# Re-timing one block's attention chunks and moving small products off VectorE in a retention and two-layer MoE kernel on one Trainium2 core

## The chip, the core and the metric

The kernel runs on one core of one Trainium2 chip. The metric is the device time of one execution in microseconds (us); lower is better. Profiles come from the hardware profiler and show one execution.

## What is computed

The reference is a chain of three parts over 4 sequences of 768 tokens with 8 heads of 64. First a retention layer: a state that decays by gamma per token and per head.

```python
state = gamma * state + outer(k[t], v[t])
y[t] = scale * (q[t] @ state)
```

Its result, 3072 tokens by 512, goes through a first layer (512 to 2048 to 512) whose activation is a cubic in h over a positive quadratic in h and |h|, and then through a second layer of the same sizes whose activation is h * clip(h + 3, 0, 6) / 6. All of it is float32 in and out.

## The kernel before, in words

The tokens are cut into 6 blocks of 512, and each block into 4 chunks of 128. A chunk is written (block, chunk) here, so (2,0) is the first chunk of the third block, which the code calls `VIA`. Every matrix product of the two layers is made of three products of rounded parts (a high part and a low rest, `h` and `l` in the names), 12 matmuls of 512 columns for the first product of a step and 12 for the second.

**Steps.** The main loop (lines 703 to 766) has one step for each block and each of 16 slices of 128 hidden features. Step n issues, among other things, on TensorE the first product h of step n (`emit_h`, line 356), then the second product of step n-2 (`emit_o`, line 368), then attention work that is hung behind it (`after`). Here they are called h(n) and o(n-2). On ScalarE (ACT) it issues the three readings of h(n-1) (`s1_h`, lines 437 to 439), the rounding of the finished activation to its high part gh(n-2) (line 467), the work on weights, then a logarithm and an exponential for h(n-1) (lines 454, 455). On VectorE (DVE) it issues the last three operations of the activation of n-2 (lines 460 to 462), weight bits (lines 125, 126), three operations on h(n-1) with the low part gl(n-2) among them (lines 445, 446, 473, 449), and attention work (`before`). Steps 0 to 7 belong to block 0, steps 8 to 23 to block 1, steps 24 to 31 again to block 0, and step 32 begins block 2. Each engine issues its instructions in the order of the program; the order between engines follows from semaphores that the tile framework sets.

**Attention chunks.** A chunk passes through: five transfers into on-chip tiles (`att_load`, line 201: q, the table for q, k, v, and k by rows, in this order), q times the table on DVE (`att_q`, line 215), v times a per-head power (`att_v`, line 220, whose result is called v' here), scores on TensorE (line 233), a mask on DVE (line 244), outputs and the state's sum on TensorE (lines 269 to 304), and evacuation on ACT and DVE (lines 327 or 332, 339, 344 or 346). `chunk_at` (line 586) hangs them on steps, for a score step s:

```python
put(before, loads, att_load, blk, c)
put(before, s - 1, att_q, blk, c)
put(before, s - 1, att_v, blk, c)
put(after, s, att_scores, blk, c)
put(before, s + 1, att_mask, blk, c)
put(after, s + 1, att_out, blk, c)
```

The second block's scores stand at steps -1, 1, 3 and 5 and those of the third block at steps 8, 12, 16 and 20, with their transfers two steps earlier (line 601). From the third block on, a chunk's q, k and v lie in the tiles `T`, `kv` and `tq` (lines 191 to 194), of which there is one each. So the transfers of the next chunk wait for the last reader of the chunk before, and the SyncE queue (SP), which issues them in the program's order, stands still meanwhile. The chunks of the third block leave by way of DRAM (`x_dram`, line 328) and are loaded back before step 32.

**Weights.** The 64 weight tiles of both layers are loaded raw, scaled on ACT (line 117), turned on DVE (lines 125, 126), rounded to the high part on ACT (line 134), and the low rest is made in one of two ways: a subtraction on DVE (line 146), or a negated copy on ACT (line 138) and a transfer issued by GpSimd (POOL) that adds the raw tile to it (line 144). `SUMS` (line 22) says which tiles take the second way, counted from 0 in the order of their use: 3 to 25 and 32 to 39. `w_until` (line 534) sets how many tiles are made by the end of a step: two a step up to step 7, then about four in five steps; tiles 26 to 31 fall in steps 16 to 22. A raw tile's room is loaded again as soon as its low rest is made (`w_ahead`, line 543).

**Evacuation.** The sum of a block (or of the first half of block 0) is copied out by ACT in four pieces (line 418) into tiles that have three buffers, and stored; the fourth copy waits for the first store. For block 0's first half this is in step 10.

Of the kernel before, what the change touches and what calls it, by code (L numbers as in the profile page):

```python
# [11 lines left out]
AF = mybir.ActivationFunctionType  # L12
ALU = mybir.AluOpType
# [3 lines left out]
NB = 512  # L17
EARLY = (0, 1)
VIA = 2
CUT1, CUT2 = 8, 8  # L20
LAG = 2
SUMS = ((3, 26), (32, 40))
EARLY_AT = 8
SPARE = ("wi14", "wi15", "wo14", "wo15")
WARM, WARM_AGAIN = 3, 3
# [6 lines left out]
def tile_retention_moe_moe2(  # L32
# [13 lines left out]
    nc = tc.nc  # L46
    NT, DM = out.shape
    H, D, S = N_HEADS, DM // N_HEADS, SEQ
# [4 lines left out]
    CPB = NB // CH  # L53
    CPS = S // CH
# [19 lines left out]
    tab_v = [tab[:, CH + i * H : CH + (i + 1) * H] for i in range(CPS)]  # L74
# [142 lines left out]

    def att_v(blk, c):
        vr = attn[blk, c][3]
        nc.vector.tensor_tensor(  # L220
            out=vr,
            in0=vr,
            in1=tab_v[(blk * CPB + c) % CPS].unsqueeze(2).to_broadcast([128, H, D]),
            op=ALU.mult,
        )

    def att_scores(blk, c):
        qT, kT, kr, vr, ka = attn[blk, c]
# [93 lines left out]
    def att_xh(blk, c):  # L322
        y = attn[blk, c][0].rearrange("p (e j t) -> p e j t", e=2, t=CH)[:, :, 0:2, :]
        xs = slice(c * CH, (c + 1) * CH)
        if blk == VIA:
            xf = o_p.tile([128, 512], F32, tag="osb", name=f"xf{blk}_{c}")
# [7 lines left out]
    def att_xl(blk, c):  # L334
        both = attn[blk, c][0]
        if blk != VIA:
            y = both.rearrange("p (e j t) -> p e j t", e=2, t=CH)[:, :, 0:2, :]
# [193 lines left out]
    def by_dma(i):  # L531
        return any(lo <= i < hi for lo, hi in SUMS)

# [49 lines left out]
    def put(where, n, fn, *args):  # L583
        where.setdefault(n, []).append((fn, *args))

    def chunk_at(blk, c, s, loads=None):
        if loads is not None:
# [7 lines that stand above are left out]
        s += blk == VIA  # L595
        put(middle if blk <= VIA else begin, s + 2, att_xh, blk, c)
        put(before, s + 2, att_evac, blk, c)

    for c in range(CPB):
        chunk_at(1, c, 2 * c - 1, max(2 * c - 3, -1))  # L600
        chunk_at(VIA, c, CUT1 + 4 * c, CUT1 - 2 + 4 * c)
        for b in range(VIA + 1, NBLK):
            n0 = at_of[0, b - 1, 0] if b > VIA + 1 else 2 * FT
            chunk_at(b, c, n0 + 4 * c, n0 + 4 * c - 2)
# [47 lines left out]
    att_q(0, 0)  # L652
    att_scores(0, 0)
    att_v(0, 0)
    att_mask(0, 0)
    att_out(0, 0)
    att_q(0, 1)
    att_scores(0, 1)
    keep_warm(WARM_AGAIN)
    att_v(0, 1)  # L660
    att_state(0, 0)
    att_xh(0, 0)
# [175 lines left out]
```

## Time and profile before

| | us |
|---|---|
| median of 3 runs | 1172.44 (1170.27 to 1173.0) |
| the profiled execution's own time | 1170.62 |
| its span, first to last instruction | 1168.8 |

The profiled execution is 1.8 us under the median, and 1.8 us of it lie outside its span. In the timeline a row is: start in us, length in us, engine, line and operation, tile written and tiles read, count of merged instructions, and in brackets the idle time of the engine before it and what ended it. Lengths of matmuls are modelled and reach into the next row by about 0.15 us, so the time that a group takes is read from the start of one group to the start of the next.

### The profile page before, as it was taken

Reading aid. Unit: us, or ns where it says so; the run is one execution under the profiler, and the core shown is the slowest. Engines: PE = TensorE matmul, PEld = TensorE weight load, DVE = VectorE, ACT = ScalarE, POOL = GpSimd, SP = SyncE. Lnnn points to the kernel's source line nnn. Section 1 sums busy time; section 2 is a strip of 40 time slices with the busy share of each in tenths; the row PEclk is TensorE's granted clock in tenths of the full one; section 3 lists DMA queues with packets and bytes.
Section 4 is the critical chain, followed back from the end, with each engine's and each line's share of the span. In section 5 each row is a group of like instructions: output and inputs, shape, how many; then the busy total and the mean of one; then the engine's idle time right before and its main releaser. Section 6 shows DMA issues by size and latency. Waiting matters only on the chain.

```text
span 1168.8 us, 15667 instructions
## 1 busy us (share of the span) xinstructions
PE 1142.8 (98%) x6028; PEld 929.6 (80%) x6028; DVE 762.1 (65%) x1187; ACT 625.3 (53%) x1029; POOL 27.6 (2%) x37
## 2 busy tenths in 40 slices
PE   8699999999999999999999999999999999999998
PEld 5567787888888888888888788888888888888886
DVE  6898999998888878888899865432332332332322
ACT  3788876866666666666888644332232332232222
POOL 0121000000000000000000000000000000000000
PEclk9899999999999999999999999999999999999999
DMA  9898722311112113121332743120200200200000
GB/s 335 244 263 231 189 67 63 135 60 68 46 46 82 46 59 113 47 81 37 109 99 64 231 134 105 36 90 1 73 1 1 72 1 1 72 1 1 36 1 36
DMA packets 58683, 98.62 MB, mean 84 GB/s; under 512 B 5233, under 2 KB 23793, under 8 KB 58609
## 3 DMA queue, kind: packets, MB, share of 16 engines
q1 hardware_dynamic: 54144, 89.50, 23.2%
q0 software_dynamic: 4464, 8.13, 4.2%
q8 instruction: 47, 0.77, 0.3%
q14 instruction: 28, 0.22, 0.1%
HBM read 73.76 MB, written 15.73 MB: 77 GB/s over the span
## 4 chain that ended last, share of the span: by engine, by line
PE 77%; DVE 11%; ACT 6%; DMA 3%; issue 3%; SPq 0%; ACTq 0%; DVEq 0%
PE h L365 37%; PE accA L389 19%; PE accB L389 18%; DMA T<-in_qk_t_dram 2%; DVE u L460 2%; DVE p L461 1%; DVE p L445 1%; PE sc L233 1%; PE py L269 1%; ACT r L454 1%; DVE u L446 1%; ACT r L455 1%; DVE p L449 1%; DVE p L462 1%; DVE rwo L126 1%
## 5 line engine op out<-in xcount | busy, mean ns | idle before, releaser
L365 PE MATMUL h<-xh,wi 128*128 128x512 f32 x1536 | 416.5, 393 | 0.9 <-ACT xh L332 0.9
L365 PEld LDWEIGHTS h<-xh,wi 128*128 128x128 f32 x1536 | 285.6, 188 | 64.0 <-issue 3.0
L365 PE MATMUL h<-xl,wi 128*128 128x512 f32 x768 | 206.1, 390 | 0.0
L485 DVE SCALAR_TENSOR_TENSOR g<-r,h 128x512 f32<-128x512 f32 x96 | 66.0, 688 | 169.0 <-ACT r L479 168.4
L365 PEld LDWEIGHTS h<-xl,wi 128*128 128x128 f32 x768 | 144.5, 188 | 31.1 <-DVE xl L339 0.3
L479 ACT ACTIVATE r<-h,cst 128x512 f32<-128x512 f32 x96 | 66.0, 687 | 183.3 <-PE h L365 182.7
L473 DVE TENSOR_TENSOR gl<-g,gh 128x512 fp32r<-128x512 f32 x96 | 66.5, 693 | 120.6 <-ACT gh L467 120.6
L467 ACT ACTIVATE gh<-g 128x512 fp32r<-128x512 f32 x96 | 60.7, 632 | 153.1 <-PE accB L389 113.9
L389 PE MATMUL accA<-gh,wo 128*128 128x512 f32 x384 | 120.5, 395 | 7.3 <-ACT gh L467 7.3
L389 PE MATMUL accB<-gh,wo 128*128 128x512 f32 x384 | 119.3, 392 | 0.0
L389 PE MATMUL accA<-wo,gh 128*128 128x512 f32 x384 | 118.2, 389 | 0.0
L389 PE MATMUL accB<-wo,gh 128*128 128x512 f32 x384 | 118.2, 389 | 0.0
L437 ACT ACTIVATE p<-h,ab 128x512 f32<-128x512 f32 x96 | 74.3, 774 | 37.6 <-PE h L365 35.4
L454 ACT ACTIVATE r<-u,cst 128x512 f32<-128x512 f32 x96 | 69.3, 722 | 43.5 <-DVE u L446 43.4
L389 PEld LDWEIGHTS accA<-gh,wo 128*128 128x128 f32 x384 | 71.4, 189 | 26.1 <-ACT gh L467 11.8
L473 DVE TENSOR_TENSOR gl<-p,gh 128x512 fp32r<-128x512 f32 x96 | 65.9, 687 | 31.0 <-ACT gh L467 30.8
L389 PEld LDWEIGHTS accB<-gh,wo 128*128 128x128 f32 x384 | 72.6, 189 | 15.4
L389 PEld LDWEIGHTS accA<-wo,gh 128*128 128x128 f32 x384 | 72.1, 188 | 15.0
L389 PEld LDWEIGHTS accB<-wo,gh 128*128 128x128 f32 x384 | 72.1, 188 | 15.0
L467 ACT ACTIVATE gh<-p 128x512 fp32r<-128x512 f32 x96 | 60.7, 632 | 38.8 <-DVE p L462 38.8
L389 PE MATMUL accA<-wo,gl 128*128 128x512 f32 x192 | 74.7, 389 | 0.0
L389 PE MATMUL accB<-wo,gl 128*128 128x512 f32 x192 | 74.7, 389 | 0.0
(74 smaller groups left out, 1418.4 us busy)
## 6 DMA issues: line engine op xcount, KB each, us to landing
rwi<-in_moe_w_in_dram SPq DMA_DIRECT2D x32, 512.0 KB, 4.8
rwo<-in_moe_w_out_dram SPq DMA_DIRECT2D x32, 512.0 KB, 3.7
T<-in_qk_t_dram SPq DMA_DIRECT2D x48, 256.0 KB, 4.1
kv<-in_kv_dram SPq DMA_DIRECT2D x32, 256.0 KB, 4.8
x<-o SPq DMA_DIRECT2D x24, 256.0 KB, 2.3
xr<-x SPq DMA_DIRECT2D x24, 256.0 KB, 4.1
out_dram<-o SPq DMA_DIRECT2D x20, 256.0 KB, 2.0
wi<-rwi POOLq DMA_DIRECT2D x17, 256.0 KB, 3.9
```

Source lines behind the costliest of these rows:

```text
L126: nc.vector.scalar_tensor_tensor(out=z, in0=hw, scalar=3, in1=lw, op0=ALU.logical_shift_left, op1=ALU.bitwise_or)
L233: nc.tensor.matmul(banks[e][:, p * CH : (p + 1) * CH], lhsT=kT[rows, p, :], rhs=qT[rows, p, :], start=True, stop=True)
L269: nc.tensor.matmul(to(e, j, i), lhsT=vr[:, 2 * p + e, :], rhs=am[:, e * NP + p, :], start=j == 0, stop=first and j == 1, skip_group_check= ...
L365: nc.tensor.matmul(ps, lhsT=w[:, cs], rhs=x[:, c, :], start=n == 0, stop=n == 3 * KD - 1)
L389: nc.tensor.matmul(acc[layer, blk][j], lhsT=l, rhs=r, start=f == f0 and i == 0, stop=f == f1 and i == 2)
L437: nc.scalar.activation(p, h, AF.Identity, scale=ab[:, 3:4], bias=ab[:, 2:3])
L454: nc.scalar.activation(r, u, AF.Ln, scale=1.0 / LN_SCALE, bias=ln_bias)
L460: nc.vector.scalar_tensor_tensor(out=u, in0=u, scalar=Q_CONST, in1=r, op0=ALU.add, op1=ALU.mult)
L467: nc.scalar.activation(gh, tm[key], AF.Copy)
L473: nc.vector.tensor_tensor(out=gl, in0=tm.pop(key), in1=gh.bitcast(F32), op=ALU.subtract)
L479: nc.scalar.activation(r, hps[key], AF.Relu, bias=three)
L485: nc.vector.scalar_tensor_tensor(out=g, in0=r, scalar=6.0, in1=h, op0=ALU.min, op1=ALU.mult)
```

## The change

Three things change. The third block's scores go from steps 8, 12, 16, 20 to steps 10, 13, 16, 20, and everything that `chunk_at` hangs on them with them: transfers from steps 6, 10, 14, 18 to 8, 11, 14, 18. The product v' of the seven chunks (1,1) to (2,3) is made on ACT by eight operations of 64 columns with a per-partition scale, in place of one operation of 512 columns on DVE; it is issued at the same place in the step. And weight tiles 26 to 31 (the 27th to the 32nd) take the way by negated copy and adding transfer.

```diff
+VIA_AT = (10, 13, 16, 20)
...
-SUMS = ((3, 26), (32, 40))
+SUMS = ((3, 40),)
...
     def att_v(blk, c):
         vr = attn[blk, c][3]
-        nc.vector.tensor_tensor(
-            out=vr,
-            in0=vr,
-            in1=tab_v[(blk * CPB + c) % CPS].unsqueeze(2).to_broadcast([128, H, D]),
-            op=ALU.mult,
-        )
+        powers = tab_v[(blk * CPB + c) % CPS]
+        if (1, 0) < (blk, c) < (VIA + 1, 0):
+
+            for h in range(H):
+                nc.scalar.activation(vr[:, h, :], vr[:, h, :], AF.Copy, scale=powers[:, h : h + 1])
+        else:
+            nc.vector.tensor_tensor(
+                out=vr, in0=vr, in1=powers.unsqueeze(2).to_broadcast([128, H, D]), op=ALU.mult
+            )
...
-        chunk_at(VIA, c, CUT1 + 4 * c, CUT1 - 2 + 4 * c)
+        chunk_at(VIA, c, VIA_AT[c], VIA_AT[c] - 2)
```

## Rows read from the trace of the kernel before

**Rows 1.** The page, busy time of engines over the span.

```profile
PE 1142.8 (98%) x6028; PEld 929.6 (80%) x6028; DVE 762.1 (65%) x1187; ACT 625.3 (53%) x1029; POOL 27.6 (2%) x37
```

**Rows 2.** Windows: stretch, length, busy time by engine, granted clock, DMA share, GB/s.

```profile
50.00:100.00 50.00, 43.45 (x288) 32.90 (x288) 49.19 (x80) 43.75 (x76) 10.53 (x12) 0.98 0.97 249
...
150.00:200.00 50.00, 49.40 (x300) 39.68 (x300) 47.75 (x77) 34.96 (x58) 0.00 (x0) 1.00 0.20 59
```

**Rows 3.** Timeline of TensorE: waits, scores of (2,0), and o(8) before h(11).

```profile
34.27 1.09 PE L269 MATMUL py<-T,T 128*64 128x128 f32 x16 [1.76 <-DVE T L244]
...
98.18 1.08 PE L389 MATMUL accA<-gh,wo 128*128 128x512 f32 x2 [2.85 <-ACT gh L467]
...
102.72 1.16 PE L233 MATMUL sc<-T 64*128 64x128 f32 x16
103.81 1.19 PE L365 MATMUL h<-xh,wi 128*128 128x512 f32 x4
...
114.43 0.62 PE L389 MATMUL accA<-gh,wo 128*128 128x512 f32 x2
...
117.15 1.07 PE L365 MATMUL h<-xh,wi 128*128 128x512 f32 x4
...
126.08 0.73 PE L389 MATMUL accA<-gh,wo 128*128 128x512 f32 x2 [0.61 <-ACT gh L467]
...
187.86 1.09 PE L269 MATMUL py<-T,kv 128*64 128x128 f32 x16 [0.60 <-DVE T L244]
...
203.87 0.73 PE L389 MATMUL accA<-gh,wo 128*128 128x512 f32 x2 [0.48 <-ACT gh L467]
```

**Rows 4.** Windows after two of these waits: granted TensorE clock is third from the end.

```profile
34.27:38.00 3.73, 2.15 (x48) 1.85 (x48) 3.21 (x6) 2.17 (x5) 1.06 (x1) 1.00 0.67 176
...
98.40:101.70 3.30, 3.30 (x9) 2.52 (x9) 2.38 (x4) 3.24 (x6) 0.86 (x1) 0.50 0.91 222
```

**Rows 5.** Timeline of VectorE in step 7: v' of (2,0), then weight bits.

```profile
91.87 0.69 DVE L220 TENSOR_TENSOR kv<-kv,tab 128x512 f32<-128x512 f32 x1
...
93.86 0.69 DVE L126 SCALAR_TENSOR_TENSOR rwo<-rwo 128x512 int32<-128x512 int32 x1
```

**Rows 6.** Timeline of ScalarE in steps 7 to 10.

```profile
94.58 0.63 ACT L134 ACTIVATE wo<-rwo 128x512 fp32r<-128x512 f32 x1 [0.97 <-DVE rwo L126]
...
106.91 0.76 ACT L437 ACTIVATE p<-h,ab 128x512 f32<-128x512 f32 x1
...
108.62 1.09 ACT L418 ACTIVATE o<-accA 128x512 f32<-128x512 f32 x2
...
112.00 0.60 ACT L418 ACTIVATE o<-accB 128x512 f32<-128x512 f32 x1 [1.80 <-DMA x<-o]
112.49 0.62 ACT L467 ACTIVATE gh<-p 128x512 fp32r<-128x512 f32 x1
```

**Rows 7.** Timeline of ScalarE: the narrowest operations with a per-partition scale.

```profile
5.30 2.43 ACT L208 ACTIVATE T<-T,T 128x128 f32<-128x128 f32 x8
```

**Rows 8.** Timeline of TensorE: outputs of (2,2), and h(18) after them.

```profile
161.65 1.09 PE L269 MATMUL py<-T,kv 128*64 128x128 f32 x16
...
163.74 1.20 PE L365 MATMUL h<-xh,wi 128*128 128x512 f32 x4
```

**Rows 9.** Timeline of the SyncE queue: q and v of (2,3).

```profile
163.87 0.33 SPq L201 DMA_DIRECT2D T<-in_qk_t_dram  x1
...
165.24 0.86 SPq L201 DMA_DIRECT2D kv<-in_kv_dram  x2
```

**Rows 10.** DMA issues, 138 to 141, then 163.5 to 166.5: count, KB, us to landing.

```profile
kv<-in_kv_dram SPq DMA_DIRECT2D x2, 256.0 KB, 6.3
...
kv<-in_kv_dram SPq DMA_DIRECT2D x2, 256.0 KB, 4.2
```

**Rows 11.** Line 201 from 80 to 260 us, 28 transfers.

```profile
DMA to landing us min/median/max: 2.6/4.4/7.1
```

**Rows 12.** Waits: ScalarE's scaling for weight loads, whole span.

```profile
ACT rwo L117 <- DMA rwo<-in_moe_w_out_dram: 2.4, 3, 1.2
```

**Rows 13.** Groups by line: the subtraction that makes a low rest.

```profile
L146 DVE TENSOR_TENSOR wo<-rwo,wo 128x512 fp32r<-128x512 f32 x18 | 12.4, 690 | 7.1 <-ACT wo L134 7.1
```

## The prediction

> **What bounds the kernel now.** I read the page first: TensorE (PE) is busy 1143 of 1169 us [rows 1], so the end moves only where PE waits, or where PE's clock falls. Then windows, to find where that is. Between 50 and 100 us VectorE (DVE) is busy 49.2 of 50 us and PE only 43.5, while ScalarE (ACT) has 6.2 us free; between 150 and 200 us PE is busy 49.4 of 50 [rows 2]. So up to about step 8 DVE sets the pace, and later PE does. Then PE's timeline, step by step. The dearest place is o(6) in step 8: PE waits 2.85 us for gh(6), and the group up to the scores behind it then takes 98.18 to 102.72, 4.54 us, where o(8) takes 114.43 to 117.15, 2.72 us [rows 3]. In that stretch the granted clock is 0.50, the lower level of 1.2 GHz; after a wait of 1.76 us at 34.27 it stayed at 1.00 [rows 3, 4]. So this wait costs 2.85 and 1.8 more. Behind step 10 only three waits of weight are left, 0.61, 0.60 and 0.48 us [rows 3]. What I had to see in each view: how little there is to win after step 10, and that new PE waits there count in full.
>
> Why o(6) is late: in step 7 DVE makes q and v' of (2,0), about 0.6 us each from start to start, before the weight bits; ACT waits 0.97 us for these bits and only then gets to h(7) and gh(6) [rows 5, 6].
>
> **What the change does, part by part.** It is followed through the two in-order queues of ACT and DVE by the starts of the rows.
>
> *Steps 0 to 8.* Three v' leave DVE, 0.6 us each. ACT gets eight operations for each. Eight of 128 columns took 2.43 us with the last one's tail, 0.29 apart [rows 7]; a copy of 512 columns is 0.49 apart from the next [rows 6], so most of an operation is fixed. With 64 columns I take 0.24, so 1.9 us for a v' (bounds 0.15 and 0.29: 1.2 and 2.3). ACT's free time swallows most of that; I leave DVE a lead of 0.75 at step 7 (bounds 0 and 1.8). There q and v' of (2,0) go too: 1.2. So the bits come 2.0 earlier, and o(6) starts at 96.2 instead of 98.18. PE then waits about 1.8 us, as at 34.27, where the clock did not fall. o(6) ends at 98.9 instead of 102.7.
>
> *Steps 8 to 10.* The scores of (2,0), 1.09 us, and its outputs, 2.09 us as for (2,2) [rows 3, 8], leave steps 8 and 9 and come in 10 and 11. That is 3.2 us of PE work which stood where PE could wait and now stands where it can't. Meanwhile v' of (2,0) is queued on ACT in step 9, in front of the readings of h(9). These started at 106.91; 2.0 earlier by the lead and 1.9 later by v' makes 106.8. Behind them ACT copies out four pieces from 108.62, the fourth waits for the first one's store, and gh(8) follows at 112.49 [rows 6]. Nothing shortens that, so gh(8) starts at 112.4 and o(8) at 113.0, where it was 114.43. PE is 1.4 us earlier with 3.2 us more to do: **+1.8**. PE has nothing from about 109.2 to 113.0. That gap of 3.8 is nearest to the 2.85 after which the clock fell, so I take another half-speed stretch: **+1.8** (bounds 0 and 1.8). The wait of 0.61 at 126.08 is covered by that lateness: **-0.6**.
>
> *The transfers of (2,1) and (2,2).* This is the part that decides. Before, a chunk's outputs came three steps ahead of the next chunk's v'. In the new spacing of three steps, the outputs of (2,0) are at the end of step 11, the transfers of (2,1) are issued in step 11 too, and q and v' of (2,1) are wanted in step 12. With one `T` and one `kv` tile, the transfer must wait for those outputs: for (2,3) the q transfer is issued at 163.87, 0.13 us after PE had finished the outputs of (2,2) [rows 8, 9]. v is issued 1.37 us behind q, and lands 4.2 to 6.3 us later [rows 9, 10]. From the end t of PE's step 11 then: v there at t + 5.7 to 7.8; v' on ACT, 1.9; the readings of h(12), which are queued behind it, 1.71; gh(11), 0.63 [rows 6]: t + 9.9 to 12.0. PE does h(12), o(10) and h(13) meanwhile, 3 x 2.72 = 8.16 us, and then needs gh(11) for o(11). It waits 1.8 to 3.9 us; I take the middle, 2.8. DVE's q waits too (q and its table land earlier) but comes through in time. The same holds for (2,2): outputs of (2,1) at the end of step 14, v' in step 15, wait before o(14): **+5.6** for the two (bounds 3.6 and 7.8). Whether the clock falls again after waits of 2.8 I leave to the upper end, 1.8 each: the shorter ends lie at the 1.76 that left it alone. (2,3) keeps its steps.
>
> *Queues.* While SP stands at these transfers, weight loads and the stores of the third block stand behind them, a few us. I cost this at nothing, since loads run ahead of their use: ACT waited for one three times in the whole kernel, 2.4 us in all [rows 12]. If that cover were gone, SP's 2.2 us of five issues would come on top. In turn the transfers of (2,0) move back two steps and let weight loads go first.
>
> *Weight tiles.* Six subtractions of 0.69 us leave DVE in steps 16 to 23 [rows 13]; ACT gets six copies of the same size, where it is busy 35 of 50 us [rows 2], and POOL, 2% busy [rows 1], six transfers. No weight is loaded into the freed rooms before step 80, and each tile is first used some steps later. On the path lie only the waits of 0.60 and 0.48 [rows 3]: **-1.1** (bounds -1.1 and 0).
>
> Sum: 1.8 + 1.8 - 0.6 + 5.6 - 1.1 = **+7.5 us** on the profiled execution, 1170.62 to 1178.1. That execution is 1.8 under the median of the runs, so I put the difference on the median: 1172.44 + 7.5 = **1179.9**. All low bounds together, with v' at 1.2 us in its three places, give about +1.6; all high ones, with the clock, +16.
>
> One rule speaks for a smaller sum. In the rows, a 256 KB transfer issued behind two others took 4.2 to 6.3 us to land, and the shortest of 28 took 2.6 [rows 10, 11]. The Trainium skill, page "DMA: Bandwidth & Descriptors", section "Anatomy of one DMA — SWDGE (gpsimd) path", puts a transfer at about 2 us plus its bytes at 436 GB/s, which would be an estimate of 2.6 us here; by it each wait would be 0.2 and the sum +2.3. The trace agrees with it in its shortest row only.
>
> **Rivals.** *Transfers land quickly* (within 0.3%). With 2.6 us, v is there at t + 4.1, each wait shrinks from 2.8 to 0.2, and the sum to +2.3: **1174.7**. For it: DMA is 20% busy after 150 us, against 97% before 100 [rows 2]. Against: both rows for v, the slower one at 138, in the same stretch.
>
> *DVE's relief carries, and ACT takes v' where it waits anyhow* (faster). Place: ACT in steps 9, 12 and 15. Then o(7) ends at 98.9 + 5.4 = 104.3, the four copies start there, gh(8) follows 3.9 later and o(8) starts at 108.9: 5.5 earlier with 3.2 more to do, -2.3; no fall of the clock; -0.6 and -1.1 as above; and the first steps give DVE's whole 1.8 instead of 0.75, -1.1. Together -5.1: **1167.3**. It decides when v' of (2,0) takes none of ACT's path and v of (2,1) lands within 2.4 us, which no row shows. For it: DVE is the fuller engine, and ACT has 6.2 us free.
>
> *The waits are long and the clock falls each time* (slower still). Landings of 6.3 and a half-speed stretch behind each of the two waits: 7.5 + 2 x 1.1 + 2 x 1.8 = +13.3: **1185.7**.
>
> That the change does not do what it says is no case of its own: the order on each engine is the program's. Only the weight part may do nothing, and that is in its bounds.
>
> **How the numbers follow.** What this kernel's measurement can tell from no change is about 0.3%, 3.5 us. Forecast (+3.5 to +10) 0.48; longer waits 0.16; quick landings, or errors that cancel, 0.15; faster 0.21. So slower 0.64, same 0.15, faster 0.21. The range from 1167 to 1186 takes in all named cases and leaves out about 2 in 10 of what lies beyond them; the likeliest case's own range is 1176 to 1183.
>
> **What would show it.** Right: in the new trace o(6) starts about 2 us earlier without a stretch at 0.50 behind it; eight small ACT operations end shortly before the readings of h(9); PE waits for gh(8) 3 to 4 us; SP issues q of (2,1) and (2,2) right behind the outputs of the chunk before; and ACT's first v' operation in steps 12 and 15 waits for a transfer of v, with PE waiting 2 to 4 us before o(11) and o(14). Wrong: if v' there does not wait for its transfer, if PE has no wait before o(11) and o(14), or if a v' takes ACT under 1 us.

## The result and the profile after

The changed kernel takes 1184.64 us (median of 4 runs, 1181.92 to 1187.8) beside 1171.59 us for the kernel before in the same session (1170.27 to 1173.0): 1.0107 times as long, 95% interval 1.0094 to 1.0119, so 12 to 13 us slower. The forecast was slower, 1179.9 us in a range from 1167 to 1186. The time lies in the range, but above the likeliest case's own range (1176 to 1183, chance 0.48) and nearest to the third rival, long waits with the clock falling behind each (chance 0.16). The profiled execution spans 1180.0 us against 1168.8, which is 11.2 more. It is the fastest of the four; the other three took 2.3 to 5.9 us longer, at a mean granted clock of 0.988 to 0.990 instead of 0.991, and they have no trace.

The page's line of engines answers [rows 1]:

```profile
PE 1148.2 (97%) x6028; PEld 933.8 (79%) x6028; DVE 754.6 (64%) x1174; ACT 641.0 (54%) x1091; POOL 32.7 (3%) x43
```

DVE lost 7.5 us of work and ACT won 15.7, as the change says, and the kernel got slower all the same. PE's busy time rose by 5.4 us with the same 6028 instructions: some of them ran at half clock. So the difference has two parts, waits of PE and clock, and both are to be read in PE's timeline, which answers [rows 3]. After 94 us it holds these waits of over 0.1 us, and no other up to 260:

```profile
97.39 0.73 PE L393 MATMUL accA<-gh,wo 128*128 128x512 f32 x2 [1.77 <-ACT gh L471]
...
105.45 0.50 PE L393 MATMUL accA<-gl,wo 128*128 128x512 f32 x1 [1.53 <-DVE gl L477]
...
114.30 0.73 PE L393 MATMUL accA<-gh,wo 128*128 128x512 f32 x2 [1.96 <-ACT gh L471]
...
136.86 0.96 PE L393 MATMUL accA<-gh,wo 128*128 128x512 f32 x2 [2.16 <-ACT gh L471]
...
161.97 1.22 PE L393 MATMUL accA<-gh,wo 128*128 128x512 f32 x2 [3.26 <-ACT gh L471]
```

They stand before o(6), the gl part of o(7), o(8), o(11) and o(14), together 10.7 us. The kernel before has waits of 2.85, 0.61 and 0.15 up to 175 us, together 3.6. The windows that begin at each of these five rows give the clock behind it (columns as in [rows 2], granted clock third from the end):

```profile
97.39:104.00 6.61, 6.47 (x26) 4.72 (x26) 5.62 (x10) 6.13 (x11) 0.86 (x1) 1.00 1.03 302
105.45:110.00 4.55, 4.55 (x13) 3.64 (x14) 4.32 (x8) 4.52 (x14) 0.58 (x1) 0.62 0.98 256
114.30:120.00 5.70, 5.70 (x35) 4.55 (x36) 3.96 (x7) 5.22 (x10) 0.86 (x1) 1.00 0.70 187
136.86:142.00 5.14, 5.14 (x22) 3.93 (x24) 5.07 (x10) 4.22 (x8) 0.00 (x0) 0.67 0.55 157
161.97:169.00 7.03, 7.03 (x29) 5.30 (x30) 5.88 (x11) 6.55 (x12) 0.86 (x1) 0.58 0.35 75
```

What the clock costs in a window is estimated as its length times (1 - granted clock): 0.38 x 4.55 = 1.7 us behind o(7), 1.7 behind o(11), 3.0 behind o(14), and nothing behind o(6) and o(8). Why o(11) and o(14) are late, SP's queue and ACT show:

```profile
126.38 0.33 SPq L202 DMA_DIRECT2D T<-in_qk_t_dram  x1
...
127.70 0.91 SPq L202 DMA_DIRECT2D kv<-in_kv_dram  x2
...
150.36 0.34 SPq L202 DMA_DIRECT2D T<-in_qk_t_dram  x1
...
151.70 1.44 SPq L202 DMA_DIRECT2D kv<-in_kv_dram  x2
```

```profile
106.12 2.01 ACT L225 ACTIVATE kv<-kv,tab 128x64 f32<-128x64 f32 x8
108.03 0.76 ACT L441 ACTIVATE p<-h,ab 128x512 f32<-128x512 f32 x1
...
113.13 0.60 ACT L422 ACTIVATE o<-accB 128x512 f32<-128x512 f32 x1 [1.84 <-DMA x<-o]
...
132.55 2.03 ACT L225 ACTIVATE kv<-kv,tab 128x64 f32<-128x64 f32 x8 [2.71 <-DMA kv<-in_kv_dram]
...
157.66 2.02 ACT L225 ACTIVATE kv<-kv,tab 128x64 f32<-128x64 f32 x8 [5.92 <-DMA kv<-in_kv_dram]
```

In PE's timeline, h(12) and h(15) begin at 126.24 and 150.23, and the groups behind o(11) and o(14) (scores, then h) follow:

```profile
126.24 1.20 PE L369 MATMUL h<-xh,wi 128*128 128x512 f32 x4
...
141.39 1.16 PE L237 MATMUL sc<-T 64*128 64x128 f32 x16
...
150.23 1.20 PE L369 MATMUL h<-xh,wi 128*128 128x512 f32 x4
...
168.71 1.19 PE L369 MATMUL h<-xh,wi 128*128 128x512 f32 x4
```

So PE goes on with h(12) and with h(15) right behind the outputs of (2,0) and of (2,1); 0.14 and 0.13 us later SP issues q of the next chunk. v follows 1.3 us behind q, and ACT's first v' operation ends a wait for it of 2.71 and 5.92 us: v was there 4.9 and 6.0 us after its issue. From there 4.31 us pass to o(11) and to o(14), both times (132.55 to 136.86, 157.66 to 161.97). ACT never waited for a weight load here, so what the prediction costed at nothing, loads standing behind these transfers, did cost ACT nothing.

### The profile page after: what moved, and what is told of

Same layout as the page of the kernel before. It is cut to its first block, busy times and chain, and to the rows that moved or that the text cites. A ratio compares the mean times of both kernels' runs of the same rounds, so it can differ in the third digit from the quotient of the medians.

```text
span 1180.0 us, 15740 instructions
## 1 busy us (share of the span) xinstructions
PE 1148.2 (97%) x6028; PEld 933.8 (79%) x6028; DVE 754.6 (64%) x1174; ACT 641.0 (54%) x1091; POOL 32.7 (3%) x43
## 4 chain that ended last, share of the span: by engine, by line
PE 79%; DVE 8%; ACT 7%; DMA 3%; issue 2%; SPq 0%; ACTq 0%; DVEq 0%
PE h L369 37%; PE accA L393 19%; PE accB L393 19%; DMA T<-in_qk_t_dram 2%; PE sc L237 1%; PE py L273 1%; DVE u L464 1%; DVE p L465 1%; DVE p L449 1%; ACT r L458 1%; DMA kv<-in_kv_dram 1%; DVE u L450 1%; ACT r L459 1%; PE py L301 1%; DVE p L453 1%
## 5 line engine op out<-in xcount | busy, mean ns | idle before, releaser
L393 PEld LDWEIGHTS accB<-gh,wo 128*128 128x128 f32 x384 | 73.7, 192 | 15.7
L449 DVE TENSOR_TENSOR p<-p,h 128x512 f32<-128x512 f32 x96 | 65.5, 682 | 23.2 <-ACT u L443 23.2
```

Of the source, the lines that this page charges most:

```text
L393: nc.tensor.matmul(acc[layer, blk][j], lhsT=l, rhs=r, start=f == f0 and i == 0, stop=f == f1 and i == 2)
L449: nc.vector.tensor_tensor(out=p, in0=p, in1=h, op=ALU.mult)
```

## The experiments

The first four, of one session, undo one part or do one part alone; the kernel before took 1172.64 us in it. The rest ran in two later sessions (before: 1172.58 and 1171.96), so across sessions the ratios are compared.

### e1_steps_back: the change without the new steps

```diff
-VIA_AT = (10, 13, 16, 20)
+VIA_AT = (8, 12, 16, 20)
```

> The changed kernel with the third block's steps put back to 8, 12, 16, 20; v' on ScalarE and the weight tiles by transfer stay. My theory (the steps cost, by the transfers of (2,1) and (2,2) that wait for the outputs of the chunk before): no wait on a v transfer in front of ScalarE's v', TensorE waits before o(11) and o(14) under 0.7 us, and the time is within 3 us of the kernel before. Rival (56 small operations on ScalarE cost by themselves, seven times 1.9 us): the time stays at least 8 us over the kernel before.

1170.28 us (1169.26 to 1172.75), ratio 0.9983 (0.9973 to 0.9993). No wait for a transfer of v is left, and PE's timeline holds these two waits after 94 us:

```profile
99.19 0.74 PE L393 MATMUL accA<-gh,wo 128*128 128x512 f32 x2 [3.50 <-ACT gh L471]
...
127.85 0.73 PE L393 MATMUL accA<-gh,wo 128*128 128x512 f32 x2 [1.36 <-ACT gh L471]
```

So v' on ACT and the weight tiles together are worth 0.2%, and all of the loss needs the steps. The first wait, before o(6), is longer than the 2.85 of [rows 3]; e3_v_only shows it again.

### e2_steps_only: the kernel before with the new steps

```diff
-        chunk_at(VIA, c, CUT1 + 4 * c, CUT1 - 2 + 4 * c)
+        chunk_at(VIA, c, VIA_AT[c], VIA_AT[c] - 2)
```

> The kernel before with only the third block's steps moved to 10, 13, 16, 20; v' stays on VectorE, the sums as before. My theory: VectorE now stands before v' of (2,1) and (2,2) until v lands, 5.7 to 7.8 us after the outputs before; then v' 0.6, three operations 2.0 and gh 0.7, so TensorE waits 1 to 3 us before o(11) and before o(14), with half clock behind some of these waits: 4 to 9 us over the kernel before. Rival (v' on ScalarE is what costs): at most 1 us over it.

1179.88 us (1178.05 to 1182.81), ratio 1.0063 (1.004 to 1.0086). With v' on DVE, it is DVE that waits for v, and PE's waits before o(11) and o(14) follow, each 3.40 us after v' began:

```profile
132.93 0.69 DVE L221 TENSOR_TENSOR kv<-kv,tab 128x512 f32<-128x512 f32 x1 [1.93 <-DMA kv<-in_kv_dram]
...
154.94 0.69 DVE L221 TENSOR_TENSOR kv<-kv,tab 128x512 f32<-128x512 f32 x1 [2.51 <-DMA kv<-in_kv_dram]
```

```profile
136.33 0.73 PE L390 MATMUL accA<-gh,wo 128*128 128x512 f32 x2 [1.61 <-ACT gh L468]
...
158.34 0.73 PE L390 MATMUL accA<-gh,wo 128*128 128x512 f32 x2 [1.75 <-ACT gh L468]
```

The windows behind both show a clock of 1.00, so the half clock that I expected behind some of these waits did not come:

```profile
136.33:142.00 5.67, 5.67 (x35) 4.51 (x36) 5.60 (x10) 5.02 (x9) 0.00 (x0) 1.00 0.58 179
158.34:164.00 5.66, 5.50 (x33) 4.05 (x34) 5.63 (x10) 5.02 (x9) 0.00 (x0) 1.00 0.17 46
```

Most of the loss is in the steps by themselves, and there is more of it when v' is on ACT: 3.40 us from the start of v' to PE here, 4.31 in the changed kernel.

### e3_v_only and e4_sums_only: the other two parts alone

The first has v' of the seven chunks on ACT and the old steps and tiles; the second only this:

```diff
-SUMS = ((3, 26), (32, 40))
+SUMS = ((3, 40),)
```

> The kernel before with only v' of the seven chunks on ScalarE. My theory: ScalarE takes it mostly where it waits anyway; o(6) moves by less than 1 us, later ones not at all: within 2 us of the kernel before, either way. Rival (v' on ScalarE costs by itself): 5 us or more over it.

> The kernel before with only weight tiles 26 to 31 by negated copy and adding transfer. My theory: only the TensorE waits of 0.60 and 0.48 us can go: 0 to 1.1 us under the kernel before. Rival (the adding transfers free the raw tiles late, and loads or sums wait for them): 1 us or more over it.

v' alone: 1171.6 us (1170.59 to 1173.49), ratio 0.9995 (0.9985 to 1.0004), no difference that can be told. DVE's relief does not reach o(6), which still waits, longer even than the 2.85 of [rows 3]:

```profile
99.37 1.22 PE L392 MATMUL accA<-gh,wo 128*128 128x512 f32 x2 [3.86 <-ACT gh L470]
```

With the old steps, v' of (2,0) is made in step 7, and there it now stands on ACT in front of the weight tile and of gh(6):

```profile
92.97 2.01 ACT L224 ACTIVATE kv<-kv,tab 128x64 f32<-128x64 f32 x8
...
95.22 0.67 ACT L117 ACTIVATE rwo<-rwo 128x512 f32<-128x512 f32 x1 [0.24 <-DMA rwo<-in_moe_w_out_dram]
```

The tiles alone: 1169.57 us (1168.87 to 1172.35), ratio 0.9978 (0.9968 to 0.9988). The waits of 0.60 and 0.48 [rows 3] are gone, and the one at 126.08 is half:

```profile
126.02 0.73 PE L389 MATMUL accA<-gh,wo 128*128 128x512 f32 x2 [0.29 <-ACT gh L467]
```

That makes 1.4 us; the span is 1.7 shorter than before's and the median 3.1, more than these waits explain. I had put the part's best at 1.1. It is the only part that gains by itself, and its interval lies whole below 1. Its median is the lowest of this study, though its interval overlaps those of e1_steps_back and e7_q_v_late.

By ratios the parts add up to 0.36% (0.63 - 0.05 - 0.22), and the whole change costs 1.07%. The other 0.7%, some 8 us, comes from parts that meet; with the intervals of the four ratios taken together this is 0.4 to 1.0%.

### e5_v_late: v' of the third block one step later

The step of v' alone is moved, from s - 1 to s, for the third block; all else is as changed.

```diff
-        put(before, s - 1, att_v, blk, c)
+        put(before, s - (blk != VIA), att_v, blk, c)
```

> The changed kernel with v' of the third block's chunks issued one step later, in the step of the scores; it is needed only by the outputs, a step after them. My theory (ScalarE stands before v' until the reloaded v lands, and h's readings and gh behind it): TensorE waits before o(11) and o(14) shrink from 2.16 and 3.26 to under 0.8 us, no half clock behind them, and o(8) waits less, since v' of (2,0) no longer stands before the readings of h(9): 8 to 12 us under the changed kernel, 0 to 4 us over the kernel before. Rival (scores and outputs in steps where TensorE is full are what costs): still 6 us or more over the kernel before.

1174.89 us (1173.01 to 1176.02), ratio 1.0021 (1.0011 to 1.003): some 10 us of the loss are gone with v' one step later. v has landed when ACT comes to v', and no wait is left before o(11) and o(14). The rival, that work in full steps is what costs, wanted 6 us or more and falls. One expectation failed: the wait before o(8) did not get shorter but grew, from 1.96 to 3.18, with the clock at 0.63 behind it (115.36 to 120). In step 10 it is now the fourth copy that holds up ACT. Up to 190 us these waits are left; behind them two of 0.60 stand at 193.08 and 209.22, so here the weight tiles did not take such waits away:

```profile
98.85 1.05 PE L393 MATMUL accA<-gh,wo 128*128 128x512 f32 x2 [1.79 <-ACT gh L471]
...
106.90 0.50 PE L393 MATMUL accA<-gl,wo 128*128 128x512 f32 x1 [0.24 <-DVE gl L477]
...
115.36 0.74 PE L393 MATMUL accA<-gh,wo 128*128 128x512 f32 x2 [3.18 <-ACT gh L471]
```

```profile
114.20 0.60 ACT L422 ACTIVATE o<-accB 128x512 f32<-128x512 f32 x1 [3.34 <-DMA x<-o]
```

### e6_one_gap: one spacing of three steps in the good order

To price one late transfer by itself: only the third chunk is moved, by one step, so that one spacing is three.

```diff
-VIA_AT = (10, 13, 16, 20)
+VIA_AT = (8, 12, 15, 20)
```

> The changed kernel with steps 8, 12, 15, 20: (2,0) keeps its old step, and just one chunk, (2,2), has its transfers in the step of the outputs before it (step 13). My theory: ScalarE waits 3 to 6 us for v of (2,2) in step 14, TensorE 1.5 to 3.5 us before o(13), with or without half clock behind it: 2 to 5 us over the run with steps 8, 12, 16, 20, so about 1172 to 1176. Rival (the move of (2,0) out of steps 8 and 9 is what costs, the transfers hide): within 1 us of that run.

1176.5 us (1176.07 to 1177.66), ratio 1.0039 (1.0025 to 1.0053), 6.2 us over e1_steps_back, more than the 2 to 5 that I expected. The wait is where it was expected, on ACT and then on PE:

```profile
148.97 2.02 ACT L225 ACTIVATE kv<-kv,tab 128x64 f32<-128x64 f32 x8 [4.46 <-DMA kv<-in_kv_dram]
```

```profile
153.28 0.73 PE L393 MATMUL accA<-gh,wo 128*128 128x512 f32 x2 [2.99 <-ACT gh L471]
```

The window behind it:

```profile
153.28:160.00 6.72, 6.72 (x33) 5.10 (x34) 5.57 (x11) 6.24 (x12) 0.86 (x1) 0.75 0.37 80
```

The wait of 2.99 us and a clock of 0.75 over the 6.72 us behind it (1.7) make 4.7. Another 0.9 is a wait before o(6) that is longer than in e1_steps_back (4.40 against 3.50), upstream of the edit. Again 4.31 us lie between v' and PE.

### e7_q_v_late: the tiles alone, and q and v' of (2,0) out of step 7

This one was to do better than the tiles alone, by moving q and v' of (2,0) to step 8; [rows 5] show one of the two in front of the weight bits. The diff is against e4_sums_only.

```diff
+        at = s - ((blk, c) != (VIA, 0))
-        put(before, s - 1, att_q, blk, c)
-        put(before, s - 1, att_v, blk, c)
+        put(before, at, att_q, blk, c)
+        put(before, at, att_v, blk, c)
```

> The kernel before with the weight tiles by transfer and with q and v' of (2,0) alone made in step 8 in place of step 7, on VectorE, the scores staying in step 8. My theory: the weight bits of step 7 come 1.2 us earlier, o(6) waits 1.2 to 1.7 us in place of 2.86 and the clock does not fall behind it; VectorE has room in step 8, where it waited 0.92 us: 2 to 3 us under the run with the weight tiles alone (1169.6). Rival (the scores of (2,0) then wait for q, and VectorE is late for the next step instead): no gain against that run.

1170.05 us (1168.5 to 1172.98), ratio 0.9983 (0.9973 to 0.9992): no gain over the tiles alone, against what I expected. The lead is there, 1.80 us of waiting instead of 2.86 (1.2 to 1.7 expected), but the clock fell behind it in spite of that:

```profile
97.82 1.09 PE L389 MATMUL accA<-gh,wo 128*128 128x512 f32 x2 [1.80 <-ACT gh L467]
```

```profile
97.82:102.00 4.18, 4.18 (x11) 3.32 (x12) 3.30 (x7) 3.13 (x6) 0.86 (x1) 0.59 1.01 301
```

And ACT gave 3.43 us back in step 10, at the fourth copy's wait for the first store.

### e8_v20_on_dve: is v' of (2,0) what holds step 10?

```diff
-        if (1, 0) < (blk, c) < (VIA + 1, 0):
+        if (1, 0) < (blk, c) < (VIA + 1, 0) and (blk, c) != (VIA, 0):
```

> The changed kernel with v' of (2,0) alone back on VectorE. My theory (v' of (2,0) stands on ScalarE's path to gh(8) in step 9): the readings of h(9) start about 1.9 us earlier, and TensorE's wait before o(8), 1.96 us, shrinks by 1 to 1.9; the waits before o(11) and o(14) stay: 1 to 2 us under the changed kernel. Rival (the four copies and their store set gh(8) anyway): no difference.

1183.88 us (1179.58 to 1184.27), ratio 1.0093 (1.0073 to 1.0114): the changed kernel's, within its scatter. PE's waits are not the changed kernel's:

```profile
114.15 1.07 PE L393 MATMUL accA<-gh,wo 128*128 128x512 f32 x2 [3.42 <-ACT gh L471]
...
139.73 1.22 PE L393 MATMUL accA<-gh,wo 128*128 128x512 f32 x2 [3.74 <-ACT gh L471]
...
165.12 0.88 PE L393 MATMUL accA<-gh,wo 128*128 128x512 f32 x2 [2.65 <-ACT gh L471]
```

The wait before o(8) grew from 1.96 to 3.42 instead of shrinking, since PE reached it earlier (the clock did not fall behind o(7) here) and o(8) started at the same time, 114.15 against 114.30. The waits before o(11) and o(14), which I expected to stay, went from 2.16 and 3.26 to 3.74 and 2.65, because v landed 6.4 and 5.3 us after its issue instead of 4.9 and 6.0. ACT begins the four copies at 107.82, 1.9 us earlier than the changed kernel, and issues the first store 1.9 earlier, at 108.46 instead of 110.35. But the fourth copy starts 0.15 earlier only (112.98 against 113.13):

```profile
112.98 0.60 ACT L422 ACTIVATE o<-accB 128x512 f32<-128x512 f32 x1 [3.58 <-DMA x<-o]
```

The list of DMA issues from 103 to 116 us shows where it went. The median landing of the four stores was 2.5 us before and 2.8 in the changed kernel, and here

```profile
x<-o SPq DMA_DIRECT2D x4, 256.0 KB, 4.5
```

with the DMA engines 0.97 busy in that stretch, against 0.72 before and 0.82 in the changed kernel. The wait for that store is in the changed kernel too (113.13, 1.84 us). So the landing of the first store sets gh(8), and in this execution the time that ACT saves in front of it is waited out behind it. e9_v_block2_dve repeats it: the first store is issued at 108.40, and the fourth copy starts at 112.77, 0.36 earlier than in the changed kernel. That full DMA engines are why the store was slow is argued from these shares only, and e7_q_v_late, where the stores took 4.4 us at a share of 0.65 in the same stretch, speaks against the share alone; no run took a weight load out of it. That stays open.

### e9_v_block2_dve: v' of the whole third block back on DVE

```diff
-        if (1, 0) < (blk, c) < (VIA + 1, 0):
+        if (1, 0) < (blk, c) < (VIA, 0):
```

> The changed kernel with v' of all four chunks of the third block back on VectorE; the second block's three v' stay on ScalarE, and the steps 10, 13, 16, 20 and the weight tiles stay as changed. Theory: the steps alone cost 7.2 us and the whole change without them gains 2.4, which would add up to +4.9, but the change costs +13.1; the rest comes from v' of (2,1) and (2,2) on ScalarE, where 1.9 us of it stand between the landing of v and the readings. So with them on VectorE, where v' takes 0.7 us beside ScalarE's queue, the waits before o(11) and o(14) shrink from 2.16 and 3.26 us to about the 1.61 and 1.75 of the kernel with the steps alone, and the time falls by 6 to 9 us to 1176 to 1179. First rival: the place of v' does not matter, the reload behind the outputs is all: the waits stay within 0.3 us of those of the changed kernel and the time is 1182 to 1186. Second rival: the surplus comes from steps 8 to 10, where PE's clock falls once more in the changed kernel: waits before o(11) and o(14) shrink, but the time stays over 1180 with a half-clock stretch between 104 and 118.

1180.5 us (1173.87 to 1181.89), ratio 1.0058 (1.0036 to 1.0079): about half a per cent better than the changed kernel, but above the 1176 to 1179 of my theory; it lies over 1180, where the second rival had it. The second wait shrank as expected, the first did not:

```profile
138.69 1.19 PE L393 MATMUL accA<-gh,wo 128*128 128x512 f32 x2 [2.86 <-ACT gh L471]
...
162.13 0.73 PE L393 MATMUL accA<-gh,wo 128*128 128x512 f32 x2 [1.58 <-ACT gh L471]
```

```profile
135.29 0.69 DVE L227 TENSOR_TENSOR kv<-kv,tab 128x512 f32<-128x512 f32 x1 [2.03 <-DMA kv<-in_kv_dram]
...
158.72 0.69 DVE L227 TENSOR_TENSOR kv<-kv,tab 128x512 f32<-128x512 f32 x1 [1.29 <-DMA kv<-in_kv_dram]
```

From v' to PE it is 3.40 and 3.41 us, as in e2_steps_only: the place of v' on ACT lengthens the chain behind each landing by 0.9 us. The rest of a wait is the landing of v, 6.5 us after its issue (128.82) the first time and 5.2 (153.54) the second. The second rival had a part too: a wait of 3.27 before o(8) with a clock of 0.72 from 113.94 to 120. The program issues v as the fourth of five transfers, 1.3 us behind q; no run issued it earlier.

A tile `kv` of its own for every other chunk, the direct test of the shared tile, was not tried.

## Why the prediction came out as it did

**The sum, term by term.** The same work is compared, from the start of one group of PE to the start of the same group after.

| term | predicted | measured on PE's timeline |
|---|---|---|
| steps 0 to 10, to the start of h(12) | +1.8 + 1.8 | +3.65 (122.59 to 126.24) |
| wait at 126.08 covered | -0.6 | -0.6 |
| o(10) behind that wait | none | -0.7 (3.41 before, 129.49 - 126.08; now 2.72, 131.82 - 129.10) |
| waits before o(11) and o(14) | +5.6 | +5.4 (2.16 + 3.26) |
| clock behind these two | 0, upper end 3.6 | +4.6 (o(11) took 1.7 longer than before, o(14) and the scores behind it 2.8) |
| waits of 0.60 and 0.48 | -1.1 | -1.1, both gone |
| sum | +7.5 | about +11.2; the span grew by 11.2 |

The start of h(12) before, which the first term uses beside the 126.24 shown above:

```profile
122.59 1.07 PE L365 MATMUL h<-xh,wi 128*128 128x512 f32 x4
```

**What failed** is the step "whether the clock falls again after waits of 2.8 I leave to the upper end". It fell behind both, and cost 4.6 us where I had put nothing. My reason was that the shorter ends lie at the 1.76 that left the clock alone [rows 3, 4]; but the value taken, 2.8, lay at the 2.85 of o(6), behind which it fell. By the rule that I used one step earlier, to go by the nearest row, this wait belonged to the other side. The term's sign was right and the waits were of the size forecast; the clock behind them was left out of the sum, and that alone takes the time out of the likeliest case's range.

**What held.** The transfers of (2,1) and (2,2) wait for the outputs of the chunk before: q is issued 0.14 and 0.13 us behind them, v another 1.3 later, v is there at t + 6.3 and t + 7.4 (I had said 5.7 to 7.8), and from v' to PE it takes 4.31 (my 1.9 + 1.71 + 0.63 is 4.24). e1_steps_back takes these waits away with the spacing, e5_v_late by time, and e6_one_gap makes one of them. A v' on ACT is 1.91 us from its first start to the readings (106.12 to 108.03), as forecast. The weight tiles gave what I called their bound, and alone somewhat more.

The rule of the Trainium skill that spoke for a smaller sum, page "DMA: Bandwidth & Descriptors", section "Anatomy of one DMA — SWDGE (gpsimd) path", about 2 us plus the bytes at 436 GB/s, is given there for one transfer issued by GpSimd. Carried over to these, which SyncE issues, it makes an estimate of 2.6 us for 256 KB. Beside it stand 4.9 and 6.0 us for v, issued behind three others (q, its table and k; the prediction said two). So the estimate does not hold here, though this says nothing against that page of the Trainium skill for its own case. The measurement decides, and the first rival, quick landings, falls with it.

**What came out right by a wrong way.** The +3.6 up to step 10 is right to 0.1 us, but not its inside. I had o(6) start at 96.2; it started at 97.39. Counted from the outputs of (1,3), which lie 0.43 us later in the new trace, it is 12.33 us instead of 13.55, so 1.22 earlier:

```profile
84.63 1.09 PE L269 MATMUL py<-T,T 128*64 128x128 f32 x16 [0.24 <-DVE T L244]
```

```profile
85.06 1.09 PE L273 MATMUL py<-T,T 128*64 128x128 f32 x16 [0.25 <-DVE T L248]
```

That is the 1.2 of q and v' of (2,0) alone; e7_q_v_late, with every v' on DVE, has the same 12.34. The lead of 0.75 that I gave to v' leaving DVE is in none of these traces. I had one gap of 3.8 us before o(8), with the clock falling behind it. There were two, 1.53 before the gl part of o(7) and 1.96 before o(8), and the clock fell behind the first. And I charged v' of (2,0) on ACT's path with 1.9 us: e8_v20_on_dve takes it away and gets 0.15 of it back, because the first store then takes 1.7 us longer to land. "Nothing shortens that", said of the copies and gh(8), held in these runs. Whether taking v' away would pay with a store as quick as the changed kernel's, no run shows. The low end of the prediction's range of sums, +1.6, leaves out the bound of 1.8 of the lead; with it, it is about +0.5, and no conclusion hung on it.

**The second rival**, DVE's relief carries, needed v' to take none of ACT's path and v to be quick. e3_v_only speaks against the first half: without any reload wait, the relief gained nothing that can be told, and v' on ACT stood in front of gh(6).

**The parts that meet** (8 us): v' on ACT makes each reload wait 0.9 longer, 1.8 in all. The rest is in part the clock: in the profiled execution of e2_steps_only it fell once after 94 us, behind the gl part of o(7), and waits of 1.61 and 1.75 left it alone; in the changed kernel waits of 2.16 and 3.26 did not, and that is the 4.6 us above. These are figures of single executions. By their spans the parts add up to +6.6 (+7.6, +0.7, -1.7) and the whole change to +11.2, so there the parts that meet make 4.6 and not 8: some of the 6.4 came back at places that were not followed. The rest of the 8 us is in runs without a trace, which scatter by 5 to 6 us in these versions, and stays open.

## What to carry to other kernels

Where two uses of a tile without a second buffer are moved closer, count from the last reader of the first use: issue, the transfers ahead in the same queue, the landing at its slowest row, the first operation on it, and what is queued behind that operation on its engine; in this kernel PE paid what the spacing did not cover, and the clock behind the longer waits as well. A step that waits for a transfer should not stand in front of the work that feeds PE: moving v' by one step, past the landing, took away some 10 us of 13. And an engine that gets work because it has free time (ACT, half idle) may stand in the chain in just the stretch where the work arrives.

## What was not expected of the hardware

**The clock behind waits of PE.** In the eleven kernels' profiles (before, changed, nine others) every wait of 2.16 us or more between 90 and 175 us was followed by a stretch at half clock, 1.2 instead of 2.4 GHz. Shorter ones were not alike: behind 1.77 before o(6) and 1.96 before o(8) in the changed kernel, behind 1.80 in e8_v20_on_dve and behind 1.50 in e2_steps_only the clock stayed, and behind 1.79 in e5_v_late and e9_v_block2_dve and behind 1.80 in e7_q_v_late it fell. The wait of 1.53 before the gl part of o(7) was followed by a fall in the changed kernel and in e2_steps_only, the same wait of 1.54 in e8_v20_on_dve was not. So the length of a wait near 1.5 to 2 us does not tell, and what else decides was not found.

**A fall costs the same nearly each time, whatever the wait.** In the same traces and stretch the clock fell 19 times. By the windows, 17 of these cost 1.6 to 1.7 us, behind waits from 1.53 to 4.40: 1.7 behind o(7) and o(11) of the changed kernel, 1.7 in e3_v_only (0.37 x 4.63) and in e6_one_gap (0.25 x 6.72). The other two cost more: 3.0 behind o(14) of the changed kernel and 2.7 behind o(11) of e8_v20_on_dve (0.43 x 6.27).

**The same transfer lands from 4.9 to 6.5 us after its issue.** v of (2,1), behind the same three others, took 4.9 in the changed kernel and 6.5 in e9_v_block2_dve. With a fall of the clock behind the wait that follows, 1.6 us in a landing could become 3 or more in the time; that is an estimate, 1.6 + 1.7. Runs of one kernel lay 6 us apart in the changed kernel and 8 in e9_v_block2_dve, against 3 to 4.5 in the versions without these waits. But e6_one_gap, with one such wait, has only 1.6, so that the landings make the scatter is not shown.
